# Batch 1's k re-laid by head pair, beside its q, and whole-pair kv products in an attention and bilinear FFN kernel

## The chip, the cores and the metric

The kernel runs on one core of a Trainium2 chip. The metric is the device time of one execution in microseconds (us), the median of a few runs. A profile is one execution of the same program, recorded by the hardware; its span is the time from the first instruction to the last. TensorE (PE) multiplies matrices and loads its weights with a separate part (PEld); VectorE (DVE) and ScalarE (ACT) do the elementwise work; GpSimd (POOL) and SyncE (SP) mostly issue DMAs here.

## The reference, cut to what matters

```python
def _attn_ref(q, k, v, g_norm):              # (8, 8, 576, 64): batch, head, token, dim
    kv = np.einsum('bhsd,bhse->bhde', k, v)
    out = np.einsum('bhsd,bhde->bhse', q, kv)
    rms = np.sqrt(np.mean(out * out, axis=-1, keepdims=True) + 1e-06)
    return out / rms * g_norm

def _moe_ref(x, w_a, w_b, w_out):            # x: (4608, 512), d_ff 1536
    return (x @ w_a) * (x @ w_b) @ w_out
```

For each batch and head a 64x64 block kv is formed from k and v over the 576 tokens, q is multiplied by it, and the result is normalised over its 64 columns. The heads of a token side by side are a row of x, which goes through two weight matrices, an elementwise product and a third matrix.

## The kernel before, in words

**Tiling.** The 4608 tokens go through the feed-forward part in blocks of 512. The first block is done in the plain way ("standard block", lines 403, 414 and 418: 12 column groups of d_ff, each with four products of 512 columns for w_a and four for w_b, an eviction on ScalarE and a multiplication on VectorE). The other eight are done with a seven-product scheme on half blocks ("units", line 868), which needs sums and differences of the weights, made by VectorE (line 775). Behind each block stands the product with w_out (line 1040).

**Attention.** Heads are taken in four pairs of two. Batches 0 and 1 ("early") are loaded by GpSimd DMAs (line 243) as 96 rows of 6 tokens each, batch 1 in two halves of four heads, in the order q, k, v, between the slices of w_a and w_b (lines 309 and 310). For a pair of an early batch the kernel makes:
- the transpose of q on TensorE (line 349 for batch 1, line 357 for batch 0), copied out by VectorE or ScalarE (line 364);
- kv: a product of k and v for each head (line 333), accumulated over the six token groups, copied by ScalarE into the diagonal of a 128x128 block `kvd` (lines 342 and 343);
- two score products of 288 tokens with that block (line 369), squares on ScalarE (line 379), sums over the head's columns by a product with ones (line 383), reciprocal roots on ScalarE (line 387), and the normalised result on VectorE into `xp` (line 392).

For batch 1, q is first re-laid by head pair on VectorE (`by_pair`, line 275): from [head, group, dim] to [group, head, dim], so that the two heads of a pair stand side by side as 128 columns and one transpose handles the whole pair. k was not: its products are made head by head, 12 of 64 columns for a pair, and two pairs are put into one step of 24.

**What sets the order.** The program is written as nodes with an engine, an assumed duration, a priority, dependencies and buffers taken and freed. `Plan.order()` lists them by simulated time, and each engine's instructions are emitted in that order. `EARLY_AT` and `W_AT` hold the assumed landing times of the early loads and of the weight slices. Each engine then works its queue strictly in order, with semaphores for what it needs. PSUM has eight banks: 0 to 3 are shared by the feed-forward products, 4 belongs to the block output, and 5 to 7 are shared by the attention's steps in two rings of at most two each (`RQ` for transposes and scores, `RS` for kv and sums).

**Around the change.** TensorE works on the standard block from about 15.5 to 42.4 us, with batch 1's steps between its products. Four products of the first unit (line 868) are put ahead as well. Batch 1's pairs 0 and 1 come at about 21 to 31 us, pairs 2 and 3 at 31 to 42 us. The w_out matrix `wo_t` is loaded much later, by a GpSimd DMA that stands behind the transposed load of batch 2's q.

Of the kernel before, what the change touches and what calls it, by code (L numbers as in the profile page):

```python
# [9 lines left out]
BF16 = mybir.dt.bfloat16  # L10
# [127 lines left out]
def kernel(  # L138
# [11 lines left out]
    nc = tc.nc  # L150

    B, H, S, D = q.shape
# [5 lines left out]
    NP = H // 2  # L158
    NE = 2
    EC, EP = 6, S // 6  # L160
# [31 lines left out]
    def sb(name, shape, dt):  # L192
        return const.tile(shape, dt, name=name)
# [5 lines left out]
    wo_t = sb("wo_t", [128, FC, d_model], FP16)  # L199
# [18 lines left out]
    EW = H * EC * D  # L218
# [11 lines left out]
    def carve(where, n, dt=BF16):  # L230
        a = arenas[where]
        w = n * (2 if dt == FP32 else 1)
        assert a[1] + w <= a[0].shape[1], (where, a[1], w)
        ap = a[0][:, a[1] : a[1] + w].bitcast(dt)
        a[1] += w
        return ap

    def early_view(ap):
        return ap[0:EP, 0 : H * EC * D].rearrange("p (h c d) -> p h c d", h=H, d=D)

    def early_load(t, b, hs):
# [6 lines left out]
    early = [  # L248
        {"q": early_view(carve("w", EW)), "k": early_view(carve("s", EW)), "v": early_view(carve("s", EW))},
        {n: early_view(carve("u" if n == "v" else "x", EW)) for n in "qkv"},  # L250
    ]

    raw = {}
    for n, src, eng, home in zip("qkv", (q, k, v), (nc.scalar, nc.sync, nc.sync), "woo"):
        t = carve(home, 2 * EC * D, FP32)[0:EP].rearrange("p (h c d) -> p h c d", h=2, d=D)
# [15 lines left out]

    q_pairs = carve("O", EW)[0:EP].rearrange("p (a c h d) -> p a c h d", a=NP, c=EC, d=D)

    def by_pair(p):
        nc.vector.tensor_copy(
            q_pairs[:, p].rearrange("p c h d -> p h c d"), early[1]["q"][:, 2 * p : 2 * p + 2]
        )

    zt = carve("b", 512)
# [10 lines left out]
    for i in range(2):  # L290
        t = const.tile([128, NP, 128], BF16, name=f"kvd{i}")
# [32 lines left out]
    class Attn:  # L324
# [3 lines left out]

        def early_kv_mm(self, p, ps):
            t = early[self.b]  # L330
            for hl in range(2):
                for c in range(EC):
                    nc.tensor.matmul(
                        ps[hl * D : (hl + 1) * D, 0:D],
                        lhsT=t["k"][:, 2 * p + hl, c, :],
                        rhs=t["v"][:, 2 * p + hl, c, :],
                        start=(c == 0),
                        stop=(c == EC - 1),
                    )

        def early_kv_out(self, p, ps, cp):
            nc.scalar.copy(self.kvd[0:D, p, 0:D], ps[0:D, 0:D])
            cp(self.kvd[D:, p, D:], ps[D:, 0:D])

        def early_qT_mm(self, p, ps):
            pq = ps[:].bitcast(BF16)
# [96 lines left out]
    plan = Plan({"PE": 5.7, "DVE": 3.3, "ACT": 2.7, "SP": 5.0, "POOL": 22.5, "V": 0.0})  # L443
# [6 lines left out]
    RQ, RS = Ring(PA, 2), Ring(PA, 2)  # L450
# [20 lines left out]
    def slices(at, win, extra):  # L471
        w0, w1 = win
        for i in range(2 * NP):
            p, h = divmod(i, 2)
            pr = w0 + (w1 - w0) * i / (2 * NP)
            x, s = ((Buf(RX), Buf(RY)) if at.b == 0 and i % 3 == 1 else (Buf(RQ), Buf(RS)))
            sq, rs = Buf(RSQ), Buf(RRS)
            ta = at.b * S + h * HF
            war = [
                n  # L480
                for j, (a, b) in enumerate(blocks_of)
                if a < ta - R + HF and b > ta - R
                for n in readers.get(j, ())
            ]
            n1 = plan.add(
                "PE", mm_us(1, HF), pr,
                lambda p=p, h=h, x=x: at.x_mm(p, h, x.tile), extra(p), [x], at.qt,
            )
            n2 = plan.add(
                "ACT", act_us(HF), pr, lambda p=p, h=h, b=sq: at.sq_op(p, h, b.tile[:, 0:HF]), [n1], [sq]  # L490
            )
            n3 = plan.add(
                "PE", mm_us(1, HF), pr,
                lambda p=p, h=h, s=s: at.s_mm(p, h, s.tile), [n2], [s], [sq],
            )
            s_done[at.b] = n3
            n4 = plan.add(
                "ACT", act_us(HF, True), pr,
                lambda p=p, h=h, b=rs: at.rs_op(p, h, b.tile), [n3], [rs], [s],
            )  # L500
            normed[at.b, p, h] = plan.add(
                "DVE", dve_us(HF) + 0.06, pr,
                lambda p=p, h=h: at.xt_op(p, h), [n4] + war + ([g_n] if at.b == 0 else []), (), [x, rs],
            )

    def early_batch(b, win):
        at = Attn(b)
        at.qt = [Buf(RKD).take()]
        at.kvd = at.qt[0].tile
        w0, w1 = win  # L510
        done = {}
        for p in range(NP):
            pr = w0 + (w1 - w0) * (p - 0.7) / NP
            sq, sk = (Buf(RX), Buf(RY)) if b == 0 else (Buf(RQ), Buf(RS))
            got = {n: plan.at(t) for n, t in zip("qkv", EARLY_AT[b][p])}
            if b == 0 and p == 0:
                for n in "qkv":
                    cast, eng, us = (
                        (nc.scalar.copy, "ACT", 0.75) if n == "k" else (nc.vector.tensor_copy, "DVE", 0.55)
                    )  # L520
                    got[n] = plan.add(
                        eng, us, pr - 1,
                        lambda n=n, cast=cast: cast(early[0][n][:, 0:2], raw[n]),
                        [got[n]],
                    )
            if b == 1:
                got["q"] = plan.add("DVE", 0.4, pr - 0.5, lambda p=p: by_pair(p), [got["q"]])
            n1 = plan.add(
                "PE", 0.25 if b else 0.45, pr, lambda p=p, s=sq: at.early_qT_mm(p, s.tile), [got["q"]], [sq]
            )  # L530
            cp, eng, us = (nc.scalar.copy, "ACT", 0.56) if p % 2 and b else (nc.vector.tensor_copy, "DVE", 0.38)
            n2 = plan.add(
                eng, us, pr, lambda p=p, s=sq, cp=cp: at.early_qT_out(p, s.tile, cp),
                [n1], (), [sq],
            )
            if b == 0:
                n3 = plan.add(
                    "PE", 0.40, pr, lambda p=p, s=sk: at.early_kv_mm(p, s.tile),
                    [got["k"], got["v"]], [sk],
                )  # L540
            elif p % 2 == 0:
                sk2 = Buf(RS)
                n3 = plan.add(
                    "PE", 0.8, pr,
                    lambda p=p, s=sk, s2=sk2: (at.early_kv_mm(p, s.tile), at.early_kv_mm(p + 1, s2.tile)),
                    [got["k"], got["v"]], [sk, sk2],
                )
            else:
                sk = sk2
            n4 = plan.add(  # L550
                "ACT", 0.45, pr,
                lambda p=p, s=sk: at.early_kv_out(p, s.tile, nc.scalar.copy), [n3], (), [sk],
            )
            done[p] = [n2, n4]
        slices(at, win, lambda p: done[p])
# [608 lines left out]
    for b in range(2, B):  # L1164
        t = b * S / N0
# [11 lines left out]
        "DVE", 0.08, 8.5, lambda: nc.vector.tensor_copy(g_col, gb.tile[:, 0:1]), [g_in], (), [gb]  # L1177
    )
    early_batch(0, (4.0, 16.0))
    early_batch(1, at_win[1])  # L1180
    ab, muls, reads = std_block((st[0], st[1]))
    wsum = weight_sums(44.0, reads)
# [18 lines left out]
    order, t = plan.order(), 5.7  # L1201
    for n in order:
        if n.eng == "PE" and n.start < 22.0:
            dummies(int((n.start - t - 0.03) * 2370))
            t = n.end
# [31 lines left out]
```

## Time and profile before

| what | value |
|---|---|
| median of 3 runs | 295.16 us (294.81 to 295.21) |
| the profiled execution's own time | 295.21 us |
| its span | 293.4 us |
| TensorE busy | 286.9 us (98%), 2624 products |
| VectorE busy | 243.2 us (83%) |
| ScalarE busy | 190.9 us (65%) |
| GpSimd busy | 77.4 us (26%) |
| kv products of batch 1 (line 333) | 48, starting from 23.8 to 33.6 us |
| re-lays of q (line 275) | 4, median 354 ns |
| mean DMA rate over the span | 124 GB/s; about 194 GB/s from 8 to 40 us |

How to read it: a busy share is an average over stages with different limits. The page shows the span in slices, the chain of work that ended last (followed back from the last instruction, at each step to what released it), and groups of instructions by line. The trace behind it can be asked for a timeline of any window, in which equal instructions that follow each other are merged into one row, with the idle time before it and what ended that.

### The profile page before, as it was taken

Reading aid. Unit: us, or ns where it says so; the run is one execution under the profiler, and the core shown is the slowest. Engines: PE = TensorE matmul, PEld = TensorE weight load, DVE = VectorE, ACT = ScalarE, POOL = GpSimd, SP = SyncE. Lnnn points to the kernel's source line nnn. Section 1 sums busy time; section 2 is a strip of 40 time slices with the busy share of each in tenths; the row PEclk is TensorE's granted clock in tenths of the full one; section 3 lists DMA queues with packets and bytes.
Section 4 is the critical chain, followed back from the end, with each engine's and each line's share of the span. In section 5 each row is a group of like instructions: output and inputs, shape, how many; then the busy total and the mean of one; then the engine's idle time right before and its main releaser. Section 6 shows DMA issues by size and latency. Waiting matters only on the chain.

```text
span 293.4 us, 6722 instructions
## 1 busy us (share of the span) xinstructions
PE 286.9 (98%) x2624; PEld 237.3 (81%) x2624; DVE 243.2 (83%) x447; ACT 190.9 (65%) x395; POOL 77.4 (26%) x96
## 2 busy tenths in 40 slices
PE   7999999999999999999999999999999999999994
PEld 3645558864788898899988998899988888888884
DVE  5454989997877988798988999979989958698964
ACT  3757766884489677867756866686859546655511
POOL 8945830850390660290000910000000000000000
PEclk9999999999999999999999999999999999999999
DMA  8999999799999699499916999340135000300044
GB/s 179 200 198 200 196 158 171 102 169 167 242 129 158 104 193 171 46 126 209 189 27 124 162 166 181 80 146 19 39 87 166 0 2 0 145 2 0 3 144 142
DMA packets 112643, 36.26 MB, mean 124 GB/s; under 512 B 89060, under 2 KB 108516, under 8 KB 112612
## 3 DMA queue, kind: packets, MB, share of 16 engines
q0 software_dynamic: 77552, 18.44, 66.7%
q1 hardware_dynamic: 34448, 16.70, 25.9%
q10 hardware_dynamic: 612, 0.71, 0.8%
q8 instruction: 20, 0.33, 0.4%
q14 instruction: 11, 0.09, 0.1%
HBM read 37.75 MB, written 14.75 MB: 179 GB/s over the span
## 4 chain that ended last, share of the span: by engine, by line
PE 81%; DMA 7%; DVE 5%; POOL 4%; issue 1%; ACT 0%; DVEq 0%; ACTq 0%; POOLq 0%
PE bk L868 46%; PE bk L1040 25%; DMA u<-in_v_dram 4%; DMA wa_t<-in_moe_w_a_dram 4%; PE bk L975 3%; PE bk L403 2%; DVE c L887 2%; PE bk L653 2%; POOL as L243 1%; PE bk L568 1%; PE bk L369 1%; PE bk L383 1%; DVE abt L925 1%; POOL so L243 1%; DVE xp L392 1%
## 5 line engine op out<-in xcount | busy, mean ns | idle before, releaser
L887 DVE TENSOR_TENSOR c<-bk,u 128x512 f16<-128x512 f32 x144 | 96.4, 685 | 21.3 <-PE bk L868 14.3
L436 ACT COPY u<-bk 128x512 f32<-128x512 f32 x144 | 81.4, 591 | 35.2 <-PE bk L868 28.1
L868 PE MATMUL bk<-xp,wa_t 128*128 128x256 f16 x288 | 55.0, 273 | 0.1
L868 PE MATMUL bk<-xp,wb_t 128*128 128x256 f16 x288 | 55.0, 273 | 0.0
L868 PEld LDWEIGHTS <-wa_t 128*128 128x128 f16 x384 | 37.0, 98 | 5.6 <-issue 0.6
L1040 PEld LDWEIGHTS <-abt 128*128 128x128 f16 x384 | 37.6, 98 | 4.4
L868 PEld LDWEIGHTS <-wb_t 128*128 128x128 f16 x384 | 37.5, 98 | 4.4
L1040 PE MATMUL bk<-wo_t,abt 128*128 128x256 f16 x288 | 37.1, 273 | 0.0
L436 ACT CAST c<-bk 128x512 f16<-128x512 f32 x48 | 28.1, 586 | 13.5 <-PE bk L868 13.0
L868 PE MATMUL bk<-T,sa 128*128 128x256 f16 x192 | 36.6, 273 | 0.0
L868 PE MATMUL bk<-T,sb 128*128 128x256 f16 x192 | 36.6, 273 | 0.0
L925 DVE TENSOR_TENSOR abt<-c 128x1024 f16<-128x1024 f16 x48 | 32.8, 685 | 0.9
L868 PEld LDWEIGHTS <-sa 128*128 128x128 f16 x288 | 27.9, 98 | 3.8 <-issue 0.3
L868 PEld LDWEIGHTS <-sb 128*128 128x128 f16 x288 | 28.2, 98 | 3.3
L1040 PEld LDWEIGHTS <-as 128*128 128x128 f16 x288 | 28.1, 98 | 3.3
L392 DVE SCALAR_TENSOR_TENSOR xp<-bk,g_col,rs 128x288 f16<-128x288 f32 x40 | 20.3, 514 | 9.7 <-ACT rs L387 9.7
L1072 ACT COPY o_sb<-bk 128x512 f32<-128x512 f32 x30 | 17.6, 585 | 16.5 <-PE bk L1040 15.9
L1040 PE MATMUL bk<-so,as 128*128 128x256 f16 x192 | 25.2, 273 | 0.0
L387 ACT ACTIVATE rs<-bk,eps_t 128x288 f32<-128x288 f32 x40 | 20.0, 505 | 6.0 <-PE bk L383 5.8
L696 POOL DMA_DIRECT2D k_t<-in_k_dram x24 | 21.2, 899 | 1.2 <-DMA u<-in_v_dram 0.9
L690 POOL DMA_DIRECT2D scr<-in_q_dram x12 | 19.6, 1636 | 1.9 <-issue 1.2
L1078 DVE TENSOR_TENSOR o_sb<-bk,o_sb 128x512 f32<-128x512 f32 (+1 forms) x26 | 16.6, 645 | 2.7 <-PE bk L1040 2.5
(109 smaller groups left out, 427.7 us busy)
## 6 DMA issues: line engine op xcount, KB each, us to landing
out_dram<-o_sb SPq DMA_DIRECT2D x20, 256.0 KB, 2.4
scr<-in_q_dram POOLq DMA_DIRECT2D x12, 288.0 KB, 7.8
k_t<-in_k_dram POOLq DMA_DIRECT2D x24, 128.0 KB, 8.8
v_t<-in_v_dram POOLq DMA_DIRECT2D x6, 512.0 KB, 10.9
out_dram<-o_sb SPq DMA_DIRECT2D x18, 128.0 KB, 2.4
wa_t<-in_moe_w_a_dram POOLq DMA_DIRECT2D x6, 256.0 KB, 10.7
wb_t<-in_moe_w_b_dram POOLq DMA_DIRECT2D x6, 256.0 KB, 10.9
wo_t<-in_moe_w_out_dram POOLq DMA_DIRECT2D x2, 768.0 KB, 9.3
```

The costliest lines, as they stand in the source:

```text
L387: nc.scalar.activation(rs, self.s_ps[p, h][:, 0:HF], AF.Abs_reciprocal_sqrt, bias=eps_t)
L392: nc.vector.scalar_tensor_tensor(out=xcols(p, self.b * S + h * HF, HF), in0=self.x_ps[p, h][:, 0:HF], scalar=g_col, in1=self.rs[p, h], op0 ...
L436: ("ACT", act_us(n), lambda: nc.scalar.copy(*args())),
L690: nc.gpsimd.dma_start(out=scr[:, :, hl, :].rearrange("p s d -> s p d"), in_=qv[hl])
L696: nc.gpsimd.dma_start(out=kt[:, c], in_=ks[:, :, c, :])
L868: nc.tensor.matmul(ps.tile[:, i * n : (i + 1) * n], lhsT=lhs(w, sm)[:, kc, :], rhs=rhs()[:, kc, :], start=start and i == 0 and kc == 0, st ...
L887: lambda: nc.vector.tensor_add(cs(fi, h), full(ps), u.tile),
L925: nc.vector.tensor_mul(t, c[:, :, :, 0], c[:, :, :, 1])
L975: nc.tensor.matmul(ps.tile[:], lhsT=ab.tile[:, fc, g * 128 : (g + 1) * 128], rhs=wo_t[:, fc, :], start=(fc == 0), stop=(fc == FC - 1),)
L1040: nc.tensor.matmul(ps.tile[:, sub * EH : (sub + 1) * EH], lhsT=lhs(slice(j, j + 1))[:, 0, sub * 128 : (sub + 1) * 128], rhs=rhs[:, j, :], ...
L1072: lambda: nc.scalar.copy(o(fi, h), bank(X, every)), [dep], takes, frees,
L1078: nc.vector.tensor_add(o(fi, h, subs), bank(ps, subs), other)
```

## The change

k of batch 1 is now re-laid by head pair as q is: four more copies on VectorE, into 3072 elements of `wo_t`, which is not loaded until later. The kv product of a pair is then made of six products of 128 columns, weights 96x128, whose result is a 128x128 block with the two heads' blocks on its diagonal; the second head's block is therefore read from column 64 on. Each pair is a step of its own again, with an assumed duration of 0.34 us in place of 0.8 for two pairs.

```diff
+    k_pairs = wo_t[:].rearrange("p a b -> p (a b)")[0:EP, 0:EW].bitcast(BF16)
+    pairs = {"q": q_pairs, "k": k_pairs.rearrange("p (a c h d) -> p a c h d", a=NP, c=EC, d=D)}
...
-    def by_pair(p):
+    def by_pair(n, p):
         nc.vector.tensor_copy(
-            q_pairs[:, p].rearrange("p c h d -> p h c d"), early[1]["q"][:, 2 * p : 2 * p + 2]
+            pairs[n][:, p].rearrange("p c h d -> p h c d"), early[1][n][:, 2 * p : 2 * p + 2]
         )
...
         def early_kv_mm(self, p, ps):
             t = early[self.b]
+            if self.b == 1:
+                for c in range(EC):
+                    nc.tensor.matmul(
+                        ps[:, 0 : 2 * D],
+                        lhsT=pairs["k"][:, p, c].rearrange("p h d -> p (h d)"),
+                        rhs=t["v"][:, 2 * p : 2 * p + 2, c, :],
+                        start=(c == 0),
+                        stop=(c == EC - 1),
+                    )
+                return
...
-            cp(self.kvd[D:, p, D:], ps[D:, 0:D])
+            c0 = D if self.b == 1 else 0
+            cp(self.kvd[D:, p, D:], ps[D:, c0 : c0 + D])
...
             if b == 1:
-                got["q"] = plan.add("DVE", 0.4, pr - 0.5, lambda p=p: by_pair(p), [got["q"]])
+                for n in "qk":
+                    got[n] = plan.add("DVE", 0.4, pr - 0.5, lambda n=n, p=p: by_pair(n, p), [got[n]])
...
-            if b == 0:
-                n3 = plan.add(
-                    "PE", 0.40, pr, lambda p=p, s=sk: at.early_kv_mm(p, s.tile),
-                    [got["k"], got["v"]], [sk],
-                )
-            elif p % 2 == 0:
-                sk2 = Buf(RS)
-                n3 = plan.add(
-                    "PE", 0.8, pr,
-                    lambda p=p, s=sk, s2=sk2: (at.early_kv_mm(p, s.tile), at.early_kv_mm(p + 1, s2.tile)),
-                    [got["k"], got["v"]], [sk, sk2],
-                )
-            else:
-                sk = sk2
+            n3 = plan.add(
+                "PE", 0.34 if b else 0.40, pr, lambda p=p, s=sk: at.early_kv_mm(p, s.tile),
+                [got["k"], got["v"]], [sk],
+            )
```

Because the planner works with other durations, the order of the standard block's, batch 1's and the first unit's instructions on TensorE, VectorE and ScalarE shifts between 22 and 43 us. On TensorE the number of instructions falls by 24 products with their weight loads; on VectorE it grows by four copies.

## The prediction

> **What bounds the kernel now.** I read three views in this order: the chain that ended last, the timeline of 20 to 46 us, and the busy times by stretch. The page gives TensorE 98% of the span at full granted clock, which says nothing of the place that changes, so the chain comes first.
>
> ```profile
> 12.16 11.04 DMA u<-in_v_dram
> 23.49 10.96 DMA wa_t<-in_moe_w_a_dram
> 34.49 0.61 PE bk L403 x2
> ...
> 40.61 1.94 PE bk L403 x9
> 42.55 8.80 PE bk L868 x80
> ```
>
> Columns: start, length, what. Up to 34.49 us the chain runs through DMA: batch 1's v load makes room in the queue, then the fifth w_a slice is issued at 23.49 and lands at 23.49 + 10.96 = 34.45. Only from 34.49 on is it TensorE work. All that TensorE does before 34.49 is beside the chain, unless it grows past the landing.
>
> ```profile
> 22.82 1.03 PE L403 MATMUL bk<-xp,wb_t 128*128 128x512 f16 x4
> 23.77 0.66 PE L333 MATMUL bk<-u,abt 96*64 96x64 bf16 x24
> 24.54 0.11 PEld L403 LDWEIGHTS <-wa_t 128*128 128x128 f16 x2 [0.22 <-DMA wa_t<-in_moe_w_a_dram]
> ...
> 33.21 0.63 PE L333 MATMUL bk<-u,abt 96*64 96x64 bf16 x24
> 33.77 0.39 PE L868 MATMUL bk<-xp,wa_t 128*128 128x256 f16 x2
> ...
> 34.49 0.11 PEld L403 LDWEIGHTS <-wa_t 128*128 128x128 f16 x2 [0.39 <-DMA wa_t<-in_moe_w_a_dram]
> ```
>
> Columns: start, length, engine, line, operation, count, idle time and what ended it. Both kv groups of batch 1 (24 small products each) end at a wait for a weight slice. The bracket is the weight loader's idle time. TensorE itself is free from about 24.26 to 24.54 and from 34.21 (four products of 0.109 from 33.77) to 34.49, some 0.28 us each time.
>
> ```profile
> 34.50:42.38 7.88, 7.88 (x40) 3.87 (x41) 6.49 (x13) 6.08 (x14) 4.39 (x6) 1.00 2.15 168
> 42.40:52.00 9.60, 9.60 (x96) 8.62 (x95) 9.02 (x19) 6.05 (x12) 0.00 (x0) 1.00 1.55 157
> ```
>
> Columns: stretch, length, then busy time of TensorE, its loader, VectorE, ScalarE and GpSimd. After the slice has landed TensorE has no idle time until 52 us. From 34.49 to 42.39 it runs 32 products of 512 columns and 8 of 288. The timeline gives 0.216 us each for the first kind (eight from 40.66 to 42.39) and 0.1225 for the second (two from 24.99 to 25.23): 6.90 + 0.98 = 7.88. So the end moves only if the landing moves, if this stretch gets more work or a gap, or if TensorE comes late to 34.49.
>
> **The change part by part.**
>
> *Kv products: removed and added on TensorE.* Out go 48 products of 64 columns in two groups, each about 0.47 us from first to last start (0.66 less the last one's 0.19), 0.49 with the last one's own step. In front of them TensorE stands 0.09 us (the products before end at 22.82 + 4 x 0.216 = 23.68) and 0.25 us (32.96 to 33.21). In come 24 products of 128 columns. The trace has none from 96 rows with new weights each time; the nearest row is batch 2's kv on line 653: 20 products of 128x128 in 1.12 us, 0.056 each, with new weights each and the same two-headed moving operand. I take 0.056: 0.67 a group. Below, the 64-column row gives 0.0205 each; above, a 256-column product with new weights (line 868) takes 0.109. I expect no pause ahead: the six 96x128 transposes of line 349 follow a weight product after 0.216 us, the ordinary step. So a group costs 0.67 against 0.58 and 0.74 with its pause: TensorE has the same work within 0.1 us.
>
> *Order around the first group.* In the changed program's compiled order the two score products of pair 0 (line 369) stand ahead of the weight products that followed. They need pair 0's kv block, copied out by ScalarE (two copies, 0.21 each). Pair 0's last product starts at 23.68 + 5 x 0.056 = 23.96 and ends 0.22 later (line 653's duration); the copies start 0.04 after that and end at 24.64; TensorE saw such a copy 0.07 later in the trace. So the score products start at 24.71, where before weight products started at 24.54. The pause of 0.28 becomes 0.36, and TensorE is 0.16 late. From there to the first early product of unit 0 stand 32 weight products, 4 score and 4 sum products and 12 transposes: 6.90 + 0.98 + 0.51 = 8.39, to 33.10; the four early products (0.44) end at 33.54, and the second kv group at 34.21. That is 0.28 before the weights are there.
>
> *Waits inside that stretch.* Sum and score products share one ring of banks. Counted from pair 0's first score product: its square is done at 0.80 and the sum product comes at 0.89, as in the trace (24.99 to 25.88). The second sum product reuses the bank of the first, free when the reciprocal root (0.53) has read it, at 1.82; TensorE comes at 1.88. Pair 1's score product reuses a bank free after VectorE's product (0.52) at 2.35; TensorE comes at 2.43. All fit, by 0.06 to 0.09.
>
> *After 34.49.* The order holds the same 32 + 8 products, with small swaps. ScalarE now does unit 0's first eviction (0.59) ahead of the kv copies: the early products' last one ends at 33.70, the eviction at 34.33, pair 2's copies at 34.65. The score product wants them at 34.94. It fits. So the stretch stays 7.90.
>
> *VectorE.* Four re-lays of k are added (L275 copies of the same shape: 354 ns median; two in a row start 0.28 apart), 1.1 us in all. Pair 0's and 1's fall between 22.3 and 23.3, where VectorE has 1.2 us idle ahead of 23.95; pair 2's and 3's at 31.7 to 32.3, after k has landed (20.52 + 11.1 = 31.6). The weight sums behind them shift by some 0.5 us. VectorE had 1.4 us idle between 36.8 and 42 (0.29, 0.79, 0.22 and a remainder), so it is back on its old times by 42. If that cover were gone, the first combination of unit 0 would come at most 1.1 us late. TensorE reads the k copies at 33.54; they end 1.2 us earlier.
>
> *Moved queues.* SyncE's order is the same. GpSimd's is too, but its w_out load now also waits for the k copies' readers, since these live in w_out's buffer; the readers end at 34.4, and that load stands behind a transpose issued at 42.32. Cost zero.
>
> The Trainium skill speaks against two steps. Its page "TensorE: Matmul & The Clock Gate", section "Back-to-back issue gap", gives about 81 ns for a 128-column product in a stream of weight loads and products. Line 653 says 56 in this kernel; by 81 the second group would end at 34.64 and the forecast would be 0.15 us later. Its page "SBUF — State Buffer" (the box on DVE blocking DMA) says that a VectorE copy with both ports keeps GpSimd from writing descriptors. The q re-lay at 20.66 ran inside GpSimd's issue at 20.52, which took 0.72 us as the one at 11.45 did with no copy beside it; by the page the four copies would hold GpSimd 4 x 0.35 = 1.4 us, which 10.96 us of queue would hide.
>
> **Sum.** Landing 0; TensorE before it 0 (0.28 in hand); stretch after it 0; VectorE 0 at 42. The profiled execution took 295.21 (span 293.4 and 1.8 around it), 0.05 above the median of 295.16. I forecast **295.2**, own range 294.9 to 295.5 (the shown runs spread from 294.81 to 295.21).
>
> **Rivals.**
>
> *Slower: the pair products cost more than 0.056 (12%).* Place: both kv groups. With c each, the score products start at 24.43 + 5c and the second group ends at 33.26 + 17c. Under c = 0.072 the landing hides it; above, all goes into the span. At the upper bound 0.109: 35.11 against 34.49, 0.62 later, 295.8. For it: no row has 96 rows with 128 columns. Against it: line 653 differs only in rows.
>
> *Slower: the bank waits (12%).* If the reciprocal root or the copies come late by over 0.3 us in all, TensorE reaches the second group after its 0.28 in hand. Two slips of 0.3 give 0.3: 295.5.
>
> *Faster: the earlier VectorE order is carried on (8%).* From 52 to 68 us TensorE has 0.22 us idle in 16. If all of it goes: 295.0. Against it: the same instructions in the same order on all engines from 43 us.
>
> *Not what it says.* The compiled order shows full-width products and four k copies; the only thing that may not come about is the saved TensorE time, and the forecast counts none.
>
> **How the numbers follow.** Forecast 68%, rivals 12, 12 and 8. Range 294.6 to 295.9: below, the faster rival less the runs' spread of 0.4; above, the upper bound of the product. A measurement of this kernel tells some 0.2%, 0.59 us, from no change. Slower by that needs c near its bound or a bank wait of twice the size: 14%. Faster: 9%. Same: 77%.
>
> **What would show it.** Right: the w_a slice still ends its wait at 34.49 and the unit's first product behind the standard block starts at 42.39; the kv groups read about 0.056 a product, with TensorE idle some 0.3 us between kv and the slice. Wrong: a start at 34.49 that is TensorE's own (no idle time before it), sum or score products waiting for ScalarE or VectorE after 34.49, or a w_a landing that has moved.

## The result and the profile after

The changed kernel is slower: 297.16 us, median of six runs (296.78 to 297.81), against 295.20 for the kernel before beside it; ratio 1.0071, 95% interval [1.0057, 1.0086]. The forecast was 295.2 with a range up to 295.9. The profiled execution is the slowest of the six, 297.81 (span 296.0), which is 2.60 over that of the kernel before. Its line numbers are 3 to 14 higher: 275 is now 278, 333 is 336, 349 is 363, 403 is 417, 690 is 695, 868 is 873, 925 is 930 and 975 is 980.

The chain of the work that ended last, changed kernel (start, length, what):

```profile
30.29 0.45 DVE o_sb L278
30.75 0.42 DVE xp L406
31.17 1.08 DVE o_sb L278
32.34 0.41 DVE T L378
32.76 0.91 DVE wo_t L278 x2
...
38.13 0.44 DVE xp L406
38.61 0.28 PE bk L383
...
43.36 8.80 PE bk L873 x80
52.17 1.12 PE bk L658 x20
53.28 0.89 PE bk L873 x8
54.28 0.81 POOL wo_t L738
55.10 12.02 DMA wo_t<-in_moe_w_out_dram
```

Before, this chain came through the w_a load and was TensorE's alone from 34.49. Now it comes through VectorE, and one re-lay in it takes 1.08 us of the chain where the prediction had 0.35. Further on it runs through GpSimd and the w_out load, which the prediction had at nothing. So there are two places, and the timeline shows each.

```profile
28.95 3.26 POOL L695 DMA_DIRECT2D scr<-in_q_dram  x2 [0.62 <-DMA wb_t<-in_moe_w_b_dram]
...
31.09 1.31 DVE L278 COPY o_sb<-abt 96x768 bf16<-96x768 bf16 x1
...
32.46 0.43 PE L363 MATMUL bk<-ident,o_sb 96*128 96x96 bf16 x6 [0.47 <-DVE o_sb L278]
...
34.24 0.83 PE L336 MATMUL bk<-u,wo_t 96*128 96x128 bf16 x12
...
34.91 0.60 PE L417 MATMUL bk<-xp,wa_t 128*128 128x512 f16 x2
```

Columns: start, length, engine, line, operation, count, idle time before it and what ended it. Before, the q re-lays of pairs 2 and 3 were one row:

```profile
30.31 0.63 DVE L275 COPY o_sb<-abt 96x768 bf16<-96x768 bf16 x2
```

Now a product with the norm stands between them, and the q re-lay of pair 3 took 1.31 us. The transposes waited for it, the second kv group came at 34.24 instead of the forecast 33.54, and the w_a products started at 34.91, 0.42 late, with no wait in front of them: the DMA bound of 34.49 is gone. Behind them VectorE was late too, and the stretch up to the first unit's product took 8.29 instead of 7.90; one of its pauses is a score product that waits for VectorE's product with the norm:

```profile
38.61 0.28 PE L383 MATMUL bk<-T,kvd 128*128 128x288 bf16 x1 [0.18 <-DVE xp L406]
```

The first unit's product behind the standard block starts at 43.20; before, at 42.39: **0.81 us** lost, place A.

```profile
53.77 0.18 POOL L735 COPY gate_t<-qT 1x1 bf16<-1x1 bf16 x1 [12.33 <-DMA qT<-scr]
54.28 1.64 POOL L738 DMA_DIRECT2D wo_t<-in_moe_w_out_dram  x2 [0.34 <-PE bk L873]
```

```profile
67.16 1.89 PE L980 MATMUL bk<-wo_t,abt 128*128 128x512 f16 x8 [1.17 <-DMA wo_t<-in_moe_w_out_dram]
```

The first two rows are GpSimd, the third is TensorE. Before, the same three instructions read:

```profile
52.12 0.18 POOL L730 COPY gate_t<-qT 1x1 bf16<-1x1 bf16 x1 [10.79 <-DMA qT<-scr]
52.36 1.64 POOL L733 DMA_DIRECT2D wo_t<-in_moe_w_out_dram  x2
65.01 1.24 PE L975 MATMUL bk<-wo_t,abt 128*128 128x512 f16 x5
```

The gate copy waits for the transposed load of batch 2's q, which landed 11.3 us after its issue (9.8 before); then come 0.34 us that the row puts down to TensorE (k's readers, the kv groups, had ended by 35; the run `k_else` below shows that the 0.34 goes with k's place in w_out's buffer); then w_out lands at 67.11 instead of 64.36, and TensorE stands 1.17 us. Its products at this place were 2.14 us late: place B. A third loss, C, is small: at 168.85 VectorE pauses where it did not before.

```profile
167.71 0.68 DVE L892 TENSOR_TENSOR c<-bk,u 128x512 f16<-128x512 f32 x1
168.85 0.69 DVE L930 TENSOR_TENSOR abt<-c 128x1024 f16<-128x1024 f16 x1 [0.46 <-DVE c L892]
```

Before, the same product (line 925) started 0.1 after the one ahead of it:

```profile
165.60 0.68 DVE L887 TENSOR_TENSOR c<-bk,u 128x512 f16<-128x512 f32 x1
166.39 0.69 DVE L925 TENSOR_TENSOR abt<-c 128x1024 f16<-128x1024 f16 x1
```

From 170.8 on TensorE is 2.45 late, and at its last product 2.50.

### The profile page after: what moved, and what is told of

The parts are those of the page before. It is cut to its first block, busy times and chain, and to the rows that moved or that the text cites. A ratio compares the mean times of both kernels' runs of the same rounds, so it can differ in the third digit from the quotient of the medians.

```text
span 296.0 us, 6678 instructions
## 1 busy us (share of the span) xinstructions
PE 288.2 (97%) x2600; PEld 237.8 (80%) x2600; DVE 245.7 (83%) x451; ACT 191.0 (65%) x395; POOL 77.1 (26%) x96
## 4 chain that ended last, share of the span: by engine, by line
PE 81%; DMA 7%; DVE 6%; POOL 3%; issue 1%; ACT 1%; DVEq 0%; ACTq 0%; POOLq 0%
PE bk L873 44%; PE bk L1045 25%; PE bk L417 5%; DMA wo_t<-in_moe_w_out_dram 4%; DMA wb_t<-in_moe_w_b_dram 3%; PE bk L980 2%; PE bk L658 2%; DVE c L892 1%; POOL as L243 1%; PE bk L383 1%; PE bk L573 1%; PE bk L397 1%; POOL so L243 1%; DVE xp L406 1%; DVE abt L432 1%
## 5 line engine op out<-in xcount | busy, mean ns | idle before, releaser
L892 DVE TENSOR_TENSOR c<-bk,u 128x512 f16<-128x512 f32 x144 | 96.4, 685 | 21.2 <-PE bk L873 14.2
```

The source lines that it names most:

```text
L892: lambda: nc.vector.tensor_add(cs(fi, h), full(ps), u.tile),
```

## The experiments

The theories. **A**: a re-lay on VectorE that starts well inside one of GpSimd's DMA issues is held until that issue ends. **B**: the fetch of TensorE's next instructions (16 KB in one packet) has moved, because the changed program has 48 TensorE instructions fewer; it now falls on the end of the transposed load. **C**: VectorE pauses at a fixed place of its own instruction stream. The rivals: for A, that VectorE simply has 1.1 us more to do; for B, that w_out is late because its buffer now holds k.

All numbers of the 19 kernels in one table. "First unit" is the start of the first unit's product behind the standard block (42.39 before); "fetch" the start of the 16 KB packet next to the load; "load" the transposed load of batch 2's q from issue to landing (9.75 before); "wait" TensorE's wait for w_out; "store" the program's last store from issue to landing (1.81 before). These five are of the one profiled execution, whose own time stands under "profiled" (295.21 before); the median and the ratio are of all runs.

| kernel | median us | ratio, 95% interval | profiled | first unit | fetch | load | wait | store |
|---|---|---|---|---|---|---|---|---|
| changed | 297.16 | 1.0071 [1.0057, 1.0086] | 297.81 | 43.20 | 51.49 | 11.3 | 1.17 | 2.15 |
| q3_next | 297.34 | 1.0069 [1.0046, 1.0092] | 296.80 | 42.26 | 50.73 | 11.2 | 0.89 | 2.37 |
| pad24 | 297.47 | 1.0078 [1.0059, 1.0098] | 296.57 | 43.10 | 45.51 | 9.9 | 0 | 2.30 |
| q3_next_pad24 | 297.16 | 1.0055 [1.0037, 1.0073] | 297.09 | 43.78 | 45.97 | 9.7 | 0 | 2.15 |
| k_else | 297.10 | 1.0060 [1.0044, 1.0076] | 297.48 | 43.30 | 51.52 | 11.3 | 0.72 | 2.17 |
| b_q3_late | 295.30 | 0.9996 [0.9978, 1.0014] | 296.10 | 42.51 | 45.13 | 9.9 | 0 | 1.80 |
| fill24 | 297.01 | 1.0059 [1.0040, 1.0079] | 296.80 | 43.36 | 45.44 | 9.7 | 0 | 2.29 |
| q3_fill24 | 296.81 | 1.0049 [1.0030, 1.0068] | 297.03 | 43.01 | 45.52 | 9.8 | 0 | 2.17 |
| all3 | 296.96 | 1.0053 [1.0033, 1.0072] | 297.17 | 43.26 | 45.66 | 10.1 | 0 | 2.20 |
| gap24 | 296.61 | 1.0043 [1.0030, 1.0055] | 296.31 | 42.98 | 45.24 | 9.7 | 0 | 2.16 |
| q3_gap24 | 296.15 | 1.0028 [1.0019, 1.0037] | 296.15 | 42.82 | 45.38 | 10.4 | 0 | 2.16 |
| q3_gap24_dve3 | 295.63 | 1.0017 [1.0008, 1.0026] | 296.13 | 42.69 | 45.06 | 9.7 | 0 | 2.30 |
| b_dve4 | 295.16 | 1.0002 [0.9991, 1.0014] | 295.15 | 42.15 | 44.81 | 9.8 | 0 | 2.23 |
| gap12 | 297.06 | 1.0066 [1.0047, 1.0086] | 296.94 | 43.26 | 49.84 | 11.2 | 0 | 2.50 |
| b_tiny | 296.53 | 1.0043 [1.0028, 1.0058] | 296.23 | 43.43 | 51.27 | 11.3 | 0 | 1.82 |
| b_dve3 | 295.74 | 1.0013 [1.0005, 1.0022] | 295.57 | 42.27 | 44.63 | 9.9 | 0 | 2.18 |
| q3act_gap24_dve4 | 295.66 | 1.0016 [1.0002, 1.0030] | 295.47 | 42.36 | 44.69 | 9.7 | 0 | 2.23 |
| kact_gap24 | 295.65 | 1.0009 [0.9992, 1.0027] | 295.18 | 42.58 | 45.17 | 9.8 | 0 | 1.82 |
| kact | 296.34 | 1.0036 [1.0021, 1.0051] | 296.46 | 43.29 | 51.65 | 11.3 | 0.46 | 1.81 |

Names that begin with b_ are the kernel before with an edit; the others are the changed kernel with one.

### A: one re-lay moved by one place

```diff
     order, t = plan.order(), 5.7
+    order.remove(tag["q", 3])
+    order.insert(order.index(tag["q", 2]) + 1, tag["q", 3])
```

> The changed kernel with one VectorE instruction moved by one place: the q re-lay of pair 3 directly behind that of pair 2, as before. Theory A (a re-lay that starts well inside one of GpSimd's DMA issues is held to the issue's end): it starts at about 30.7, within 0.1 us of the issue's start, and takes about 0.35 instead of 1.31; the transposes of pair 3 then follow without idle time, the w_a products wait for the landing at 34.49 again, and the unit's first product comes at 42.4 instead of 43.2. Rival (VectorE simply has 1.1 us more to do): the same copies in the same 3 us, the w_a products still start near 34.9 and the unit's first near 43.2. Total: w_out's landing near 67.1 then still ends TensorE's wait there, so theory B (its load is late whatever TensorE did before) expects the wait on it to grow from 1.17 to about 1.9 us and the total to stay near 297; if the late landing is a consequence of the 0.8 us, 295.2 to 295.5.

The timeline of this run, VectorE and then TensorE:

```profile
30.10 0.82 DVE L278 COPY o_sb<-abt 96x768 bf16<-96x768 bf16 x2
...
32.09 0.63 DVE L278 COPY wo_t<-abt 96x768 bf16<-96x768 bf16 x2 [0.36 <-DMA abt<-in_k_dram]
```

```profile
33.05 0.38 PE L874 MATMUL bk<-xp,wa_t 128*128 128x256 f16 x2
33.27 0.38 PE L874 MATMUL bk<-xp,wb_t 128*128 128x256 f16 x2
33.49 0.83 PE L336 MATMUL bk<-u,wo_t 96*128 96x128 bf16 x12
34.36 0.61 PE L417 MATMUL bk<-xp,wa_t 128*128 128x512 f16 x2
```

The copy started at 30.59, 0.09 after GpSimd's issue (30.50), and took 0.34. With the same eight copies the w_a products wait for their landing again (34.31 here) and the first unit's product is at 42.26, 0.94 earlier than in the changed kernel. The rival falls: it is the place of one copy, not their sum. The wait for w_out should have grown to 1.9 and was 0.89, because the w_out load itself landed at 65.89 instead of 67.11. The median did not fall, as the theories together expected: B takes back what A gives. In the profiled runs it does so only in part: behind the wait TensorE was 0.88 late against the kernel before, where it was 2.10 late in the changed kernel, and the time was 296.80 against 297.81; the other five runs of q3_next lie between 296.44 and 298.62.

The reverse in the kernel before, the same copy one place later:

> The kernel before, with its q re-lay of pair 3 one place later on VectorE, behind one product with the norm, as the changed kernel has it; nothing else. Theory A: the copy starts near 31.0, some 0.45 us inside GpSimd's second scr issue (30.57 to 32.20), is held and ends 0.16 to 0.19 us behind that issue's end, so it takes about 1.3 us; the transposes of pair 3 start near 32.45 instead of 31.84, TensorE comes to 34.49 some 0.3 to 0.4 us late, and the total is 0.3 to 0.8 us over the kernel before: 295.5 to 296.0. Rival (the cost is VectorE's added copies, not the place of one): 295.2.

```profile
31.34 0.97 DVE L275 COPY o_sb<-abt 96x768 bf16<-96x768 bf16 x1
...
32.36 0.43 PE L349 MATMUL bk<-ident,o_sb 96*128 96x96 bf16 x6 [0.41 <-DVE o_sb L275]
```

The hold came as expected: the copy ended at 32.31, 0.19 behind the issue's end at 32.12, and TensorE stood 0.41. The price did not: the 0.28 us that TensorE has in hand ahead of the w_a landing hid all but 0.13, and the ratio is 0.9996. (The profiled run, 296.10, is the slowest of twelve for another reason, at 194 us; see "Open" below.) In the changed kernel the hold cost more, and in two steps. Against q3_next TensorE was 0.74 late at the transposes and, after the landing, 0.55 at the w_a products. VectorE, which has the k re-lays and weight sums behind the held copy and no idle time from 31.1 to 38.5, then carried 0.95 us to the product with the norm, and the score product that waits for it made TensorE 0.94 late. TensorE did not wait for the k copies themselves. So the price of a hold lies in what is in hand and in what stands behind the copy.

### B: where TensorE's instruction fetch falls

```diff
-    dummies(10 * 512)
+    for _ in range(34):
+        dummies(120)
```

> The changed kernel with 24 more warm-up products ahead of 6 us (34 of 120 columns in place of 10 of 512), so that TensorE has as many instructions ahead of 42 us as before; no other change. Theory B (the fetch of TensorE's next instructions, one 16 KB packet at 51.49 in the changed kernel and at 45.02 before, falls on the end of batch 2's transposed load): the fetch comes some 2.5 to 6 us earlier again, the transposed load lands about 9.8 us after its issue instead of 11.3, w_out lands near 65.5, TensorE's wait of 1.17 at 67.16 is gone, and of the loss only the 0.8 us at 43 us is left: 295.9 to 296.2. Rival (w_out's load is late because its buffer now holds k, with new waits on GpSimd): unchanged, 296.8 to 297.8.

The load landed after 9.9 us and the wait was gone: w_out's buffer has nothing to do with it. The median did not fall, though, and the runs spread from 296.57 to 298.33. The warm-up's own fetch had moved as well, from 14.1 to 11.9, among the first loads. With the re-lay moved too:

> Both edits at once: the q re-lay of pair 3 directly behind that of pair 2, and 24 more warm-up products. If A and B are the two causes, nothing of the loss is left: 295.2 (295.0 to 295.5), the unit's first product at 42.4 and no wait on w_out near 67. If only A holds, near 296.8; if only B holds, 295.9 to 296.2; if neither, 297.

Its runs lay from 295.69 to 298.14; in the profiled one batch 0's v landed so late that TensorE stood 0.90 at 14.10. The two edits could not be judged by this warm-up. The rival of B, k in other buffers (the first three pairs in `xt`, the fourth behind the re-laid q):

> The changed kernel with the re-laid k in other places (three pairs in a buffer that is not used before batch 5, one behind the re-laid q) instead of w_out's buffer, so that GpSimd's w_out load has no new waits. Rival of B (the new waits make w_out late): the load is issued right behind its gate again, the wait at 67 goes, 295.9 to 296.2. Theory B: the transposed load still lands late; only the 0.34 us that GpSimd stood idle ahead of the issue can come back, so the wait falls from 1.17 to about 0.85 and the total stays at 296.5 to 297.4.

The load still took 11.3, the wait was 0.72 instead of 1.17. GpSimd's idle time of 0.34 was gone and w_out landed at 66.76, 0.35 earlier. So the buffer accounts for these 0.34 and no more; this rival falls.

To leave the early fetches alone, 24 products were put behind the kv groups (`fill24`, alone, with the re-lay, and with both other edits; in these three the second twelve overwrite a 64x64 corner of the first unit's early product, so only their times count):

> The changed kernel with 12 products of 64 columns on zeros behind each of batch 1's two kv groups (24 in all, 0.02 to 0.03 us each), so that TensorE's instructions are as many as before from 34 us on, while the warm-up and its early instruction fetches stay those of the changed kernel. Theory B: the 16 KB fetch comes at about 45 to 46 instead of 51.5, the transposed load lands 9.8 us after its issue, no wait for w_out near 67; A's loss stays, and the 0.36 us of a group add at most 0.4: 295.9 to 296.4. Rival (w_out late because of k's buffer): 296.8 to 297.8.

> The q re-lay of pair 3 directly behind that of pair 2, and the 24 small products behind the kv groups. If A and B are the two causes and the wide spread of the runs with a changed warm-up came from its early fetches: 295.1 to 295.5, first unit product at 42.3 to 42.5, no wait for w_out, and a spread like that of the kernel before. If the runs spread to 297 or more again, there is a third cause in what the runs differ in.

> q re-lay of pair 3 directly behind that of pair 2, 24 small products behind the kv groups, and k in other buffers than w_out's. By A and B 295.1 to 295.5; the buffer gives nothing more than some 0.3 us in w_out's landing, which nobody waits for then.

All three took the wait away, but their second twelve stand right ahead of the w_a products, which came at 35.11 to 35.46: that was a poor place. A better one is TensorE's pause from 14.2 to 15.3, behind the first fetch:

```diff
-            dummies(int((n.start - t - 0.03) * 2370))
+            cols = int((n.start - t - 0.03) * 2370)
+            for _ in range(28 if cols > 1900 else 0):
+                nc.tensor.matmul(banks[4][0:D, 0:D], lhsT=zt[:, 0:D], rhs=zt[:, 0:D], start=True, stop=True)
+            dummies(cols if cols <= 1900 else 0)
```

> The changed kernel with the four warm-up products of TensorE's pause at 14.2 to 15.3 us replaced by 28 of 64 columns that take as long: 24 products more, behind the first instruction fetch (14.1) and ahead of all work that matters; nothing else. Theory B: the later fetches come at the times of the kernel before (27.8, 45.0 to 45.7), the transposed load lands 9.8 us after its issue, TensorE does not wait for w_out, and 0.8 (A) and 0.3 (the pause at 168 us) are left: 296.2 to 296.5, with a narrower spread than with more warm-up products ahead of 6 us. Rival (w_out late for another reason): 296.8 to 297.8.

> The same 28 small products, and the q re-lay of pair 3 directly behind that of pair 2. Theories A and B together: unit's first product at 42.2 to 42.4 as in the run with the re-lay alone, no wait for w_out, and only the pause at 168 us left: 295.3 to 295.7. If 296.5 or more, something else costs as much as B.

The medians were 296.61 and 296.15: undoing B gives back about 0.6 of the 1.96, and the moved re-lay 0.46 more, now that B no longer hides it. This 0.46 is not a clean price of A: in the profiled run of q3_gap24 the copy started 0.37 inside the issue and was held again (1.45 us), and TensorE gained only 0.16 by the move (first unit 42.82 against 42.98). So moving the copy by one place is not a sure cure.

Half the shift tells whether the fetch meets the load's end by its own time:

> The changed kernel with the four warm-up products of the pause at 14.2 to 15.3 us replaced by 16 of 112 columns: 12 products more, half of what put the fetch back to 45.2. The transposed load's packets run from 46.4 to 51.7 in all profiles. Theory B1 (the fetch comes when TensorE gets to its place): it comes half way, at about 48, and the load's end is undisturbed: landing 9.8 us after issue, no wait for w_out, as with 24: 296.4 to 296.8. Theory B2 (a fetch that is asked for while the load's packets stand in the queue waits behind them, and the load's last two small packets then wait behind the fetch): it comes near 51 and the load lands some 11.2 us after its issue, as without the 12 products: 296.9 to 297.6.

B1 falls: the load took 11.2. The fetch started at 49.84, between the two forecasts. B2 has the landing right but not the reason: here the fetch ended at 51.16, and what was late is the data, whose packets ran for 6.3 us (45.90 to 52.21) where they ran for 5.2 in the changed kernel; q3_next, with a fetch at 50.73, shows the same 6.3. (TensorE did not wait for it: its re-lay of pair 2 was held for 1.49 us, so it came to w_out at 65.88, when that had landed at 65.87.) With 24 products it starts at 45.2, ahead of the load's packets (46.4 to 51.7), and harms nothing. Where the fetch comes later, the packets show what B2 says. In the changed kernel the last of the load's 2304 data packets starts at 51.73, much as before (51.59); its last two packets of 4 bytes come at 52.67, just as the fetch packet ends (51.49 + 1.19 = 52.68). What is late is the load's last word, behind one packet of 16 KB; k_else, b_tiny and kact, with fetches at 51.27 to 51.65, show the same. The packets from 51.4 to 51.6 in the changed kernel, by queue (q1 is the load, q8 the fetch; packets, MB, share of 16 engines):

```profile
q1 hardware_dynamic: 112, 0.02, 55.2%
q8 instruction: 1, 0.02, 37.3%
```

And in the kernel before, with 104 small products more (208 instructions, the same place modulo 256):

> The kernel before with 104 more small products in TensorE's pauses ahead of 17 us (64 columns each, as many as the time of the products they replace), which is 208 instructions: with a fetch of 256 instructions, the place of the changed kernel, 48 fewer. Theory B: a fetch starts between 50.5 and 51.7, the transposed load of batch 2 lands 11 to 11.3 us after its issue instead of 9.75, w_out lands near 65.8, TensorE waits some 0.8 us for it near 65: 295.8 to 296.4; early fetches in other places may add to that. Rival (the late load belongs to the changed order of batch 1): landing 9.8, 295.2.

The fetch came at 51.27 and the load took 11.3: B can be brought about without the change. But w_out landed at 66.01, and TensorE, late by 1.05 for other reasons, was there only at 66.06: the small products had made it 0.81 late by 25 us, and the re-lay of pair 2 at 31.06 was held for 1.26. So this run shows the late load, not its price.

### C: three VectorE instructions

```diff
-    nc.vector.memset(one, 1.0)
+    for _ in range(5):
+        nc.vector.memset(one, 1.0)
```

> The kernel before with four more one-element memsets on VectorE in its first 3 us; nothing else. In all runs of changed kernels VectorE stands 0.35 us between a semaphore and the product behind it, always the same instruction (line 930, at 168.85 in the changed kernel), and TensorE's work from there on is 0.31 to 0.35 later. Theory C (the pause belongs to a place in VectorE's instruction stream, which four more instructions move): the pause comes at the same product here (line 925 at 166.4), total 0.3 up: 295.4 to 295.6. Rival (it belongs to the timing of the changed kernel): no pause there, 295.2.

> The re-lay of pair 3 early, the 28 small products, and three more one-element memsets on VectorE in its first 3 us. Theory C: the pause falls three instructions earlier in the stream, where VectorE waits for a result of its own anyway; with A and B undone too the total is that of the kernel before, 294.9 to 295.3. Rival to C: 0.3 more, as without the memsets.

With four memsets more nothing stood in the kernel before; with three more in the changed one the pause at 168 was gone, and another came at 289.31 (0.47 idle ahead of a product that otherwise has 0.10). Counted from 0, the pause in the changed kernel is ahead of record 319 of VectorE's stream, the new one ahead of record 575, 256 further on. The product of line 925 is record 316 before, and with four more 320. So three had to be tried:

> The kernel before with three more one-element memsets on VectorE in its first 3 us. The changed kernel has three records more on VectorE ahead of line 930's product at 168.85, which is its 319th; with four more the same product of the kernel before was the 320th and nothing stood. Theory C: with three it is the 319th, VectorE stands 0.35 us ahead of it near 166.4, and TensorE is 0.3 late from 168 on: 295.4 to 295.6. Rival: no pause, 295.2.

```profile
165.48 0.69 DVE L888 TENSOR_TENSOR c<-bk,u 128x512 f16<-128x512 f32 x1
166.63 0.69 DVE L926 TENSOR_TENSOR abt<-c 128x1024 f16<-128x1024 f16 x1 [0.46 <-DVE c L888]
```

The same pause of 0.46 at the same product, made by three memsets at the start: theory C holds. TensorE was 0.12 early ahead of the pause and 0.23 late behind it, so the pause costs 0.35; the median is 0.62 up, more than the pause alone.

### What is left

> The changed kernel with the q re-lay of pair 3 on ScalarE, which stands idle from 31.0 to 32.9 us, the 28 small products at 14.2, and four more memsets on VectorE (net three more records). Theory A: a copy on ScalarE is not held by GpSimd's issue: about 0.8 us from 31.0, transposes of pair 3 near 31.9, w_a products at 34.4 to 34.6, first unit product at 42.3 to 42.5; with B and C undone too, 295.0 to 295.5 with the spread of the kernel before. If 0.4 us are still missing, a fourth cause is left.

On ScalarE the copy ran from 30.86 to 31.70 inside the issue (30.55 to 32.18) without being held, and TensorE's work was within 0.03 us of that of the kernel before at 40. Still the median was 295.66, 0.5 over the kernel before and 0.16 over what was expected. The last two runs put the four re-lays of k on ScalarE, so that VectorE has its old stream again, but for one semaphore record less (576 records, 577 before):

```diff
-        nc.vector.tensor_copy(
+        (nc.vector.tensor_copy if n == "q" else nc.scalar.copy)(
```

> The changed kernel with the four re-lays of k on ScalarE (0.84 us each) in place of VectorE, whose stream is then that of the kernel before, and the 28 small products at 14.2 us. If all that the change lost is B and what it did to VectorE's stream: no held copy between 31 and 33, no pause at 168, the last store 1.8 us again, no wait for w_out; ScalarE's two copies from 32.1 to 33.8 can bring TensorE to 34.49 some 0.1 to 0.4 late: 295.1 to 295.6. If the last store takes 2.1 or more again, the rest is not VectorE's.

> The same without the small products: B alone. The fetch falls at 50 to 51.7, the transposed load lands 11.2 us after its issue, w_out lands between 65.8 and 67, TensorE comes to it at 65.0 to 65.4 and waits 0.6 to 1.7: 0.6 to 1.7 over the run with the products, 296.0 to 297.0. If B costs nothing alone, no difference between the two.

The kernel before and kact_gap24 can't be told apart (1.0009 [0.9992, 1.0027]; its profiled run 295.18). kact, the same without the small products, has B's wait:

```profile
66.54 0.81 PE L980 MATMUL bk<-wo_t,abt 128*128 128x512 f16 x3 [0.46 <-DMA wo_t<-in_moe_w_out_dram]
```

The medians of the two differ by 0.69, which is not the price of B alone. In kact's profiled run the q re-lay of pair 3 started 0.28 us inside GpSimd's issue and was held (1.54 us); in that of kact_gap24 it started 0.24 inside and took 0.35. The first unit's product came at 43.29 and 42.58. So of the 1.28 us between the two profiled runs 0.71 are A, although VectorE copies no k here, and about 0.6 are B.

No version of the change beats the kernel before.

## Why the prediction was wrong

**Right.** The kv products cost what line 653 said: the groups started at 23.73 and 34.24 with 0.056 a product, 0.67 a group, not the 81 ns that the Trainium skill gives (page "TensorE: Matmul & The Clock Gate", section "Back-to-back issue gap"). The score products of pair 0 came at 24.74 (forecast 24.71). No bank wait showed. Where the hold was taken away (q3_next) the early products came at 33.05 (33.10), the group ended at 34.16 (34.21), the w_a landing still decided, and the stretch from it to the first unit's product was 34.36 to 42.26, the forecast 7.90. TensorE's own sums held.

**The step "VectorE: four re-lays at 354 ns, 1.1 us, back on its old times by 42"** failed. One copy took 1.31; the k copies ended at 33.66 instead of 32.3, though TensorE, late itself, did not wait for them; VectorE had no idle time left to catch up in by 38.5; and the first unit's product came 0.81 late. Two of the prediction's own signs of being wrong showed: a start behind the second kv group (34.91) with no wait in front of it, and a score product that waits for VectorE (38.61). The row of 354 ns was a median of four copies, of which two started within 0.14 us of an issue's start and one 0.15 ahead of an issue's end. The fourth started 0.40 inside the issue at 20.52 and took 0.477, and I read over that. The prediction had the Trainium skill's rule (page "SBUF — State Buffer") beside it but used one half: that a VectorE copy holds GpSimd. The section "Who interferes with whom" of that page also says, of VectorE in a mode that uses both ports, that whoever issues first gets the shared ports for the whole instruction and the other blocks fully. With issues of 1.63 us and copies of 0.35, the second half is the dear one, and the runs show it: 12 copies took 0.97 to 1.54 us, held to the issue's end. The section also says that ScalarE never waits there, and the copies on ScalarE (0.83 to 0.84 inside an issue) agree.

**The step "Moved queues: cost zero"** was nearly right about the wait that it weighed (0.34 of GpSimd where it had zero, k_else) and wrong in its sum, because it asked only what the w_out load waits for, and not whether the load ahead of it would land at its old time.

**The step that failed furthest** is the sentence against the third rival, "the same instructions in the same order on all engines from 43 us". The instructions are the same, but their places in the streams are not: 48 fewer on TensorE, three records more on VectorE (four copies more, one semaphore record less). B and C come from that alone. No rival covered it, so the range could not.

**The sum.** In the profiled run: TensorE is 0.81 late at 43.20 (A), 2.14 at 67.16 (B takes over: the wait does not add to A, it swallows it), 2.45 from 170.8 (C) and 2.50 at its last product; 0.12 more come behind that, 2.6 in all. So this one run is accounted for. The prices by medians are less sharp. B: 0.55 (297.16 to 296.61, two sets of runs), where TensorE in the profiled run of gap24 is 0.59 late behind the w_out product instead of 2.10. The moved re-lay: 0.46 once B is gone, though it did not always undo A. The three memsets that undo C: 0.52 (296.15 to 295.63), though the two profiled runs, 296.15 and 296.13, do not differ: the 0.35 at 168 is gone and 0.33 is lost at 226. About 0.45 of 1.96 is left.

**Open.** That rest. Two candidates stand in the profiles. One is the 0.33 just named. ScalarE waits there for a transposed load of a later batch:

```profile
224.67 0.78 ACT L636 ACTIVATE xp<-xp,g_col 128x576 f16<-128x576 f16 x1 [0.18 <-DMA xp<-xs]
```

The same wait, at 193 to 226 us, stands in the profiles of b_q3_late, q3_fill24 and all3 (0.79, 0.55 and 0.46 of ScalarE; TensorE loses 0.80, 0.70 and 0.61), and not in those of the kernel before and of the changed kernel. Why the load was late is not shown, nor how often it is. The other is the end. From TensorE's last product to the end the profiles read 3.56 and 3.58 us in the two programs with 576 VectorE records, 3.76 to 3.78 in the three with 577, and 3.90 to 4.26 in the 15 others. It goes with the last store (1.80 to 1.82 against 2.15 to 2.50) and could hold 0.1 to 0.5 of the rest, but b_dve4 has the long store and the old median, so it is not shown to be the cause.

## What to carry to other kernels

A copy is priced by where it will start, not by the median of its kind: look at what GpSimd is issuing at that time, and at what stands behind the copy if it takes as long as the issue. When a change alters the number of instructions, every later instruction fetch moves, so for each load that something waits for, see whether a fetch can now stand inside it; equal instructions behind the change are no proof of equal times. And when two late things meet at one wait, undo both before judging either.

## What the runs showed of the hardware

- **Held copies.** In 12 of the 20 profiles a VectorE copy of 96x768 bf16 started 0.28 to 0.85 us inside GpSimd's second scr issue; each ended 0.157 to 0.189 us behind the issue's end. Copies that started up to 0.24 us inside took 0.34 to 0.36; where the start was 0.18 and 0.24 inside, the issue took 1.72 and 1.78 instead of 1.63. So GpSimd, too, can be the one that waits, and the border lies near 0.25 us behind the issue's start (0.244 inside: free, 0.283: held, by the same copy in kact_gap24 and kact). The weight sums of VectorE on fp16 that fell inside a scr issue, about one in a profile, were not longer (0.55).
- **Instruction fetches are transfers.** TensorE's come as one packet of 16 KB (0.88 to 1.86 us). Where one started in the last 2 us or so of a transposed load's packets (49.84 to 51.65), the load landed 11.2 to 11.3 us after its issue instead of 9.7 to 9.9 (six profiles against twelve; two others had 10.1 and 10.4).
- **A pause at two places 256 records apart.** VectorE paused some 0.35 us more than usual ahead of records 319 and 575 of its stream where it had nothing queued there. The Trainium skill (page "Runtime: NRT & Kernel Launch", section "Instruction fetch mechanics") says that instructions come in blocks of 256, 16 KiB, and that crossing a block is mostly hidden. The distance agrees, and it is all that ties VectorE's pause to a fetch: no run shows the fetch itself at the pause. "Hidden" does not hold here for the load behind TensorE's fetch, nor for the pause if it is one.
